# Three float32r passes in the last network's first layer, and sixteen products of zeros in the first step

## The chip, the core and the metric

The kernel runs on one core of a Trainium2 chip. The core has five engines, each with its own instruction queue that it works off in order: TensorE (PE; its weight loads are shown as PEld) multiplies matrices into PSUM; VectorE (DVE) and ScalarE (ACT) work element by element and can read and write PSUM and SBUF; GpSimd (POOL) works in SBUF only; SyncE (SP) only starts transfers. Transfers are started from SP's, ACT's and POOL's queues. Engines wait for each other with semaphores.

The metric is the device time of one execution in microseconds (us), as the median of several runs. The profile comes from one profiled execution.

## The reference

A gated linear attention (a matrix state per head that decays by a gate and takes in one outer product for each token) is followed by a two-layer network with a parametric ReLU. Batch 4, 8 heads, 768 tokens, head size 48; model size 384, inner size 2048; everything in float32.

```python
f = 1.0 / (1.0 + np.exp(-f_logit))
for t in range(S):
    state = f[:, :, t, :, None] * state + np.einsum('bhd,bhe->bhde', k[:, :, t], v[:, :, t])
    y[:, :, t] = np.einsum('bhd,bhde->bhe', q[:, :, t], state)
x = y.transpose(0, 2, 1, 3).reshape(B * S, H * D)      # 3072 x 384
h = x @ w_in                                           # 3072 x 2048
g = np.maximum(h, 0.0) + alpha * np.minimum(h, 0.0)
return g @ w_out                                       # 3072 x 384
```

## The kernel before

The 3072 tokens are cut into 12 steps: six chunks of 128 tokens, and for each chunk two pairs of batch rows (U = 2). A step is an attention part and a network part on 2 x 128 = 256 token columns.

**Attention of a step.** `loaded` fetches q, k, f and v; `scanned`, `gated`, `keyed` and others prepare decayed queries and keys on DVE and ACT; PE then makes score products (`scored` into `raw`, `scored4` into `qu`), products between half chunks (`across` into `off`), the state's increments (`pd`) and the output (`summed` into `py`). The output is copied to `y` and carried by ten transfers into `xT`, the network's input with the model dimension on the partitions (`by_token`; four of the transfers are started by ACT). In the first step there is no earlier state, and its parts (`opening`) are single letters: `r` raw scores, `o` the off products, `O` their copies to `A` by ACT, `k` the transposes `pk`, `K` their copies, `u` quarter scores `qu`, `U` and `H` their placing into `ad` by DVE and ACT, `t` copies to `A`, `y` the output product, `x` the way to `xT`.

**Network of a step.** `network` yields 13 pieces. Eight make the first layer: for each f two tiles of 128 inner rows, each as three products over the 384 model rows (`NK` = 3) of a 128x128 block of `w_in_sb` with 256 columns of `xT`, added up in one PSUM bank `ph` (L716). ACT makes `neg` = relu(-ph) (L721), DVE makes `gate` from it, `om` = 1 - alpha and ph (L723); after every fourth f DVE makes four sums `S` of halves of the gate (`sums`, L800). The other five pieces make the second layer as a 2x2 block product with seven instead of eight block products (`pa`, `pb`, `pc`, `pd`, `pe`, L755), with sums on DVE and ACT (`plus`, L759; L766, L776) and two stores. The step (0, 0) has a plain network instead (`po`, L736).

**PSUM.** The network's banks come from a pool of four (`psn`) that are used in turn: `ph0` of a network takes the bank that `pb` of the network before it had, `ph1` that of `pc`, and so on.

**Weights.** `w_in` and `w_out` arrive as raw pieces of 768 words a partition (five `raw` buffers), are converted by ACT (`a`, `b`; four `lead` buffers) and joined by DVE (`w`, `v`) in the first steps.

**Order.** PE, DVE and ACT get their instructions in the order of the list ORDER, which `flat` makes out of two strings written by hand: HEAD for the first steps, USUAL for every later one. In USUAL, `S` is a piece of `attend` of step n, `O` its `carry`, `Q` a piece of `prepare` of step n + 1, and `n` a piece of the network of step n - 1, so a network runs one step behind its attention. The last step's network runs alone at the end (USUAL with n = 12, in which only `n` is left). POOL and SP are ordered by a scheduler. Before all of it, 56 small products into the bank `idle` keep PE at work while the first data arrive (L833).

Of the kernel before, what the change touches and what calls it, by code (L numbers as in the profile page):

```python
# [7 lines left out]

F32 = mybir.dt.float32
I16 = mybir.dt.int16  # L10
F16 = mybir.dt.float16
# [3 lines left out]
AF = mybir.ActivationFunctionType  # L15
ALU = mybir.AluOpType

C = 128
DB = 32
MASKED = (1, 0)  # L20

U = 2
CH = 64
NC2 = C // CH
NB = DB // 4
WP = 768
IDLE = 56
RAWS, LEADS = 5, 4
UP = 2.0 ** 16

HEAD = (
# [8 lines left out]
)  # L40
USUAL = "S n2 S n2 O n Q n3 Q S2 n Q S n Q S n Q n Q n"

def flat(head, usual, steps=12):
    out = []
    for word in " ".join(head).split():
        if word in "awbvW":
            out.append((word, None))
        elif word[0] in "01":
            out.append((word[1:], int(word[0])))
        else:  # L50
            out.append((word[0], int(word[1:])))
    for n in range(len(head), steps + 1):
        for key in usual.split():
            for _ in range(int(key[1:] or 1)):
                k = key[0]
                m = n - 1 if k == "n" else n + 1 if k == "Q" else n
                if 0 <= m < steps:
                    out.append(("P" if k == "Q" else k, m))
    return out

ORDER = flat(HEAD, USUAL)


@with_exitstack
def kernel(
# [30 lines left out]
    nc = tc.nc  # L96
    B, NC, _, HP, _ = qT.shape
    DM = v.shape[-1]
    H = 2 * HP
    D = DM // H  # L100
    NF = alpha.shape[1]
    NK = DM // 128
# [18 lines left out]
    const = ctx.enter_context(tc.tile_pool(name="const", bufs=1))  # L121
    work = ctx.enter_context(tc.tile_pool(name="work", bufs=2))
    staging = ExitStack()
    stage = staging.enter_context(tc.tile_pool(name="stage", bufs=1))
    psa = ctx.enter_context(tc.tile_pool(name="psa", bufs=2, space=bass.MemoryType.PSUM))
# [5 lines left out]
    def bank(name):  # L131
        return psn.tile([128, 512], F32, tag="net", name=name)

# [11 lines left out]
    for bp in range(B // U):  # L145
        vs.append(const.tile([128, NC2, U, DM + 16], F32, tag=f"vs{bp}", name=f"vs{bp}"))
        nc.vector.memset(vs[bp], 0.0)

    kr = const.tile([128, W // 4, 4], F32, tag="kr", name="kr")
    nc.gpsimd.memset(kr[:, :, 3:4], 1.0)  # L150
    NS = G * (NB + 1) + 1
    fs = const.tile([128, NS], F32, tag="fs", name="fs")
    nc.gpsimd.memset(fs, 0.0)
    ones = const.tile([128, NS], F32, tag="ones", name="ones")
    nc.gpsimd.memset(ones, 0.0)
    nc.gpsimd.memset(ones[:, 0:NS:NB + 1], 1.0)
    qd = const.tile([128, G, QW], F32, tag="qd", name="qd")


    mraw = const.tile([128, 4, NB, 4], F32, tag="mraw", name="mraw")  # L160
    nc.gpsimd.memset(mraw, 0.0)
    diag = lvl[:, 1].rearrange("p (i r) -> p i r", r=4)
    for d in range(4):
        nc.gpsimd.tensor_copy(mraw[:, d, :, d:4], diag[:, :, 0:4 - d])
    inq = const.tile([128, NB], F32, tag="inq", name="inq")
    nc.vector.tensor_reduce(inq, diag, mybir.AxisListType.X, ALU.add)
    mquad = const.tile([128, UW], F32, tag="mquad", name="mquad")
    nc.gpsimd.memset(mquad, 0.0)
    for m in range(1, NB):
# [3 lines left out]
                              inq[:, 0:n].unsqueeze(2).broadcast_to((128, n, 4)))  # L173
    mhalf = const.tile([128, VW], F32, tag="mhalf", name="mhalf")
    nc.gpsimd.memset(mhalf, 0.0)
    for half in range(2):
        for m in range(1, NQ):
# [3 lines left out]
                                  inq[:, NQ * half:NQ * half + n].unsqueeze(2).broadcast_to((128, n, 4)))  # L181
    ad = const.tile([128, U, 2, HP, DB], F32, tag="ad", name="ad")
    nc.gpsimd.memset(ad, 0.0)


    A = const.tile([128, U, H, C], F32, tag="A", name="A")
    nc.gpsimd.memset(A, 0.0)
    ident = const.tile([128, 128], F32, tag="ident", name="ident")
    make_identity(nc, ident)
# [74 lines left out]
    def loaded(bp, c, x):  # L264

        i = f"{bp}_{c}"
        b0 = U * bp
        loads = nc.gpsimd if bp or c else nc.sync

        def load(name, src):  # L270
            t = work.tile([128, W], F32, tag=name, name=f"{name}_{i}", bufs=1)
            loads.dma_start(out=t.rearrange("p (u x) -> p u x", u=U),
                              in_=src[b0:b0 + U, c].rearrange("u p h t -> p u (h t)"))
            return t

        f = x["f"] = quads(load("f", fT))
        q = load("q", qT)
        x["k"] = load("k", kT)
        for cc in range(NC2):
            t_, _ = halves(cc)  # L280
            loads.dma_start(out=vs[bp][t_, cc, :, 0:DM], in_=v[b0:b0 + U, c, t_].rearrange("u t d -> t u d"))

        nc.scalar.activation(f, f, AF.Sigmoid)
        nc.scalar.copy(kr[:, :, 2:3], f[:, :, 3:4])
        nc.scalar.copy(qd[:, :, 0:DB], q.rearrange("p (g t) -> p g t", t=DB))  # L285
        by32 = "p (g i) r -> p g (i r)"

        def lagged(d):
            nc.vector.tensor_tensor(qdv[d], qdv[d - 1][:, :, :, 1:5 - d],  # L289
                                    f[:, :, 1:5 - d].rearrange("p (g i) r -> p g i r", i=NB), ALU.mult)  # L290

        nc.vector.tensor_tensor(kr[:, :, 1:2], f[:, :, 2:3], f[:, :, 3:4], ALU.mult)
        lagged(1)
        nc.vector.tensor_tensor(kr[:, :, 0:1], f[:, :, 1:2], kr[:, :, 1:2], ALU.mult)
        lagged(2)
        nc.vector.tensor_tensor(fq, f[:, :, 0:1].rearrange(by32, i=NB), kr[:, :, 0:1].rearrange(by32, i=NB), ALU.mult)
        lagged(3)
# [10 lines left out]
    def scanned(bp, c, x):  # L308

        i = f"{bp}_{c}"  # L310
        ps = work.tile([128, NS], F32, tag="ps", name=f"ps_{i}", bufs=1)
        ut = work.tile([128, G * UW], F32, tag="us", name=f"us_{i}", bufs=1)
        if c:
# [14 lines left out]
        nc.vector.tensor_tensor_scan(ps, fs, ones, 0.0, ALU.mult, ALU.add)  # L328
        ss = work.tile([128, NS], F32, tag="ss", name=f"ss_{i}", bufs=1)
        nc.vector.tensor_tensor_scan(ss[:, ::-1], fs[:, ::-1], ones[:, ::-1], 0.0, ALU.mult, ALU.add)  # L330
# [8 lines left out]
    def keyed(bp, c, x):  # L339
        i = f"{bp}_{c}"  # L340
        k4 = x["k4"] = work.tile([128, W], F32, tag="k4", name=f"k4_{i}", bufs=1)
        nc.vector.tensor_tensor(k4, x["k"], kr.rearrange("p n r -> p (n r)"), ALU.mult)
        x["k4v"] = by_four(k4.rearrange("p (g t) -> p g t", g=G))
        x["q3"] = work.tile([128, GC, 3, DB], F32, tag="q3", name=f"q3_{i}", bufs=1)
        x["ks"] = work.tile([128, GC, 2, DB], F32, tag="ks", name=f"ks_{i}", bufs=1)
        x["kh"] = work.tile([128, GC, DB], F32, tag="kh", name=f"kh_{i}", bufs=1)
        x["f32"] = x["pre"][:, :, NB:NB + 1]
        x["some"] = slice(0, GC) if c else slice(1, GC, 2)
# [15 lines left out]
    def begun(bp, c, x):  # L364
# [3 lines left out]
        started(0, x)  # L368
        f64 = x["f64"] = work.tile([128, U, H], F32, tag="f64", name=f"f64_{bp}_{c}")
        by64 = x["pre"].rearrange("p (a c j) i -> p a c j i", c=NC2, j=2)  # L370
# [336 lines left out]
    def network(bp, c, x):  # L707
        i = f"{bp}_{c}"
        xT = x["T"]
        plain = (bp, c) == steps[0]  # L710
        for f in range(NH):
            ph = bank(f"ph{f}_{i}")
# [20 lines left out]
        if plain:  # L733
# [11 lines left out]
            return  # L745

        a11, a12, a22 = (lambda f, j=j, u=u: gate[:, f, j, u * C:(u + 1) * C] for j, u in ((0, 0), (1, 0), (1, 1)))
        s1, s2, s3, s4 = (lambda f, n=n: late["S"][:, n, f] for n in range(4))
# [8 lines left out]

        def plus(to, of, by, scale=UP):
            nc.vector.scalar_tensor_tensor(to, of[:, 0:DH], scale, by, ALU.mult, ALU.add)  # L759
# [5 lines left out]
        product(pb, a22, t4)  # L765
        nc.scalar.activation(kept, pa[:, 0:DH], AF.Copy, scale=UP)  # L766
        yield
# [7 lines left out]
        plus(o0[:, DH:DM], pd, u2)  # L775
        nc.scalar.activation(o0[:, 0:DH], pa[:, 0:DH], AF.Copy, scale=UP)  # L776
        yield
        pe = bank(f"pe_{i}")
        product(pe, s4, b22)
        plus(u3, pc, kept)  # L780
        plus(o1[:, 0:DH], pb, u3, -UP)
        plus(o1[:, DH:DM], pd, u3)
# [5 lines left out]

    late = {}

    def sums(fs_):
# [10 lines left out]
    def halves_of_w_out():  # L802

        staging.close()
        pool = ctx.enter_context(tc.tile_pool(name="late", bufs=1))
        late["kt"] = pool
# [14 lines left out]

    idle = bank("idle")

    steps = [(bp, c) for c in range(NC) for bp in range(B // U)]
# [3 lines left out]

    pieces["W"] = halves_of_w_out()

    with tc.manual_schedule(engines={mybir.EngineType.PE, mybir.EngineType.DVE, mybir.EngineType.Activation}):
# [12 lines left out]
        for key, n in ORDER:  # L844
            part = pieces[key] if n is None else run[key, n]
            part() if callable(part) else next(part)


# [53 lines left out]
```

## Time and profile before

| what | value |
|---|---|
| median of 3 runs | 607.08 us (605.29 to 607.75) |
| span of the profiled execution | 604.5 us |
| 0 to 41 us | PE busy 27.5, DVE 32.2, ACT 31.3 us |
| 41 to 546 us | PE 503.0 of 505 us, DVE 447.2, ACT 211.1 |
| 546 to 562 us (second layer of network 10, last transfers to xT) | PE 16.0, DVE 1.8, ACT 1.6 |
| 562 to 583 us (first layer of the last network) | PE 21.0, DVE 9.0, ACT 4.2 |
| 583 to 604.5 us (second layer of the last network) | PE 18.2, DVE 5.5, ACT 1.3 |

The page lists groups of instructions as "line engine op out<-in xcount | busy us, mean ns of one | idle before, releaser". Records of PE overlap, so the distance from one to the next says more than the length of one. An f32 product shows as two records. A line of a timeline is "start us, length us, engine, line, op, xcount [idle before <-who ended it]"; it runs like instructions together.

### The profile page before, as it was taken

To read this page: it belongs to the slowest core of one execution; us is meant where nothing else is said; L and a number is where in the kernel's file an instruction comes from. 1 tells how busy PE (TensorE), PEld (TensorE's weight loads), DVE (VectorE), ACT (ScalarE), POOL (GpSimd) and SP (SyncE) were. 2 spreads that over 40 slices of the span, in tenths; PEclk is the share of its full clock that TensorE was granted. 3 is DMA by queue.
4 is the path that set the end of the run, shared out by engine and by line. 5 is a ranking of instruction groups with operands and counts; after the bars stand their busy time and mean duration, and the time that the engine had idled before them with its cause. 6 is when DMAs were issued, how large, how long until landed. Compare 5 with 4: busy or idle time off the path is not lost.

```text
span 604.5 us, 18724 instructions
## 1 busy us (share of the span) xinstructions
PE 585.7 (97%) x8040; PEld 526.9 (87%) x8040; DVE 495.7 (82%) x997; ACT 249.5 (41%) x478; POOL 62.8 (10%) x117
## 2 busy tenths in 40 slices
PE   5689999999999999999999999999999999999997
PEld 5678768898898899899899899799899899889997
DVE  7799999998898888889889899798798798761351
ACT  5988943712622442452452361262161363232110
POOL 8210010010010010010020020001001000000000
PEclk9999999999999999999999999999999999999999
DMA  8969132324232242232233223303314401201000
GB/s 284 359 209 381 38 88 50 76 62 104 49 88 31 81 101 38 58 104 46 61 87 63 65 54 94 66 37 97 81 36 89 90 3 30 52 2 28 27 1 27
DMA packets 68115, 50.41 MB, mean 83 GB/s; under 512 B 47168, under 2 KB 60608, under 8 KB 68032
## 3 DMA queue, kind: packets, MB, share of 16 engines
q1 hardware_dynamic: 56656, 25.01, 15.6%
q0 software_dynamic: 6864, 22.35, 13.1%
q10 hardware_dynamic: 4512, 1.85, 1.6%
q8 instruction: 64, 1.05, 0.8%
q14 instruction: 19, 0.16, 0.1%
HBM read 36.21 MB, written 4.72 MB: 68 GB/s over the span
## 4 chain that ended last, share of the span: by engine, by line
PE 90%; DVE 4%; ACT 2%; DMA 2%; SPq 1%; issue 1%; DVEq 0%; ACTq 0%
PE ph L716 40%; PE pc L755 9%; PE pa L755 9%; PE pb L755 5%; PE pe L755 4%; PE pd L755 4%; PE py L521 4%; PE po L736 4%; PE qu L498 3%; PE raw L489 3%; PE pd L436 2%; PE off L463 1%; SPq L422 1%; DMA ksn<-kt 1%; DMA f<-in_fT 1%
## 5 line engine op out<-in xcount | busy, mean ns | idle before, releaser
L716 PE MATMUL ph<-xT,w_in_sb 128*128 128x256 f32 x1152 | 257.6, 382 | 0.9 <-issue 0.9
L716 PEld LDWEIGHTS ph<-xT,w_in_sb 128*128 128x128 f32 x1152 | 216.2, 190 | 33.3 <-issue 3.1
L721 ACT ACTIVATE neg<-ph 128x512 f32<-128x512 f32 x96 | 57.0, 596 | 175.2 <-PE ph L716 136.6
L723 DVE SCALAR_TENSOR_TENSOR gate<-neg,om,ph 128x256 f32<-128x256 f32 x192 | 82.5, 477 | 41.3 <-ACT neg L721 41.1
L755 PE MATMUL pc<-t,S 128*128 128x192 f32 x352 | 61.6, 328 | 0.0
L755 PE MATMUL pa<-w_out_sb,gate 128*128 128x192 f32 x352 | 61.1, 327 | 0.0
L755 PEld LDWEIGHTS pa<-w_out_sb,gate 128*128 128x128 f32 x352 | 57.9, 190 | 0.6
L755 PEld LDWEIGHTS pc<-t,S 128*128 128x128 f32 x352 | 57.4, 190 | 0.5
L553 DVE COPY_PREDICATED ad<-mquad,qu 128x224 f32<-128x224 int32 (+6 forms) x140 | 41.9, 299 | 6.2
L506 DVE COPY_PREDICATED ad<-mraw,raw 128x256 f32<-128x256 int32 (+1 forms) x96 | 42.2, 442 | 3.2 <-PE raw L489 0.5
L380 ACT COPY A<-q 48x512 f32<-48x512 f32 x44 | 27.1, 617 | 35.5 <-DVE q L354 35.1
L513 ACT COPY A<-ad 32x256 f32<-32x256 f32 x96 | 38.8, 404 | 1.5
L776 ACT ACTIVATE o<-pa 128x192 f32<-128x192 f32 x11 | 3.6, 330 | 84.2 <-PE pa L755 77.3
L397 DVE TENSOR_TENSOR us<-us,fs 128x768 f32<-128x768 f32 (+5 forms) x60 | 36.6, 611 | 0.1
L759 DVE SCALAR_TENSOR_TENSOR Csum<-pc,Csum 128x192 f32<-128x192 f32 x22 | 7.9, 357 | 29.7 <-PE pc L755 29.3
L800 DVE TENSOR_TENSOR S<-gate 128x512 f32<-128x512 f32 x44 | 30.3, 688 | 0.8
L755 PE MATMUL pb<-t,gate 128*128 128x192 f32 x176 | 30.4, 326 | 0.0
L755 PE MATMUL pe<-w_out_sb,S 128*128 128x192 f32 x176 | 30.4, 326 | 0.0
L755 PE MATMUL pd<-w_out_sb,S 128*128 128x192 f32 x176 | 30.4, 326 | 0.0
L325 ACT COPY us<-qd 128x256 f32<-128x256 f32 x48 | 27.0, 672 | 7.4 <-DVE qd L289 4.4
L289 DVE TENSOR_TENSOR qd<-qd,f 128x768 f32<-128x768 f32 (+2 forms) x36 | 27.1, 752 | 3.2 <-ACT qd L285 3.2
L498 PE MATMUL qu<-us,k 48*32 48x112 f32 (+1 forms) x1536 | 26.1, 259 | 3.8 <-ACT ad L633 2.2
(114 smaller groups left out, 743.6 us busy)
## 6 DMA issues: line engine op xcount, KB each, us to landing
w_out_raw<-in_w_out SPq DMA_DIRECT2D x8, 767.8 KB, 8.4
w_in_raw<-in_w_in SPq DMA_DIRECT2D x8, 767.2 KB, 13.0
q<-in_qT POOLq DMA_DIRECT2D x11, 512.0 KB, 4.2
f<-in_fT POOLq DMA_DIRECT2D x11, 512.0 KB, 4.3
k<-in_kT POOLq DMA_DIRECT2D x11, 512.0 KB, 4.7
out<-o SPq DMA_DIRECT2D x24, 192.0 KB, 2.3
vs<-in_v POOLq DMA_DIRECT2D x22, 192.0 KB, 4.7
ksn<-kt SPq DMA_DIRECT2D x80, 32.0 KB, 2.0
```

The source lines that it names most:

```text
L289: nc.vector.tensor_tensor(qdv[d], qdv[d - 1][:, :, :, 1:5 - d], f[:, :, 1:5 - d].rearrange("p (g i) r -> p g i r", i=NB), ALU.mult)
L380: nc.scalar.copy(A[halves(cc)[1], :, par * HP:(par + 1) * HP, CH * cc:CH * (cc + 1)], x["q3"][rows(par)].rearrange("p (u h c) s t -> p u h ...
L397: nc.vector.tensor_tensor(by_four(us[:, :, UO[m]:UO[m] + 4 * n]), by_four(us[:, :, skip:skip + 4 * n]), spread(fq[:, :, 1:1 + n], n), ALU. ...
L498: nc.tensor.matmul(qu[DB * j:DB * (j + 1), par, hp * QS + 4:hp * QS + QL], lhsT=x["k4"][r_, g * DB:(g + 1) * DB], rhs=x["us"][r_, g, 4:QL] ...
L506: nc.vector.copy_predicated(adu[:, :, :, d:4], mraw[:, d, :, d:4].bitcast(I32).unsqueeze(1).broadcast_to((128, H, NB, n)), rv[:, :, QO[d]: ...
L513: nc.scalar.copy(A[s_, u, :, s_], ad[s_, u].rearrange("p r h t -> p (r h) t"))
L553: nc.vector.copy_predicated(ad[:, u, :, :, 4 * m:DB], mquad[:, lo:lo + n].bitcast(I32).unsqueeze(1).unsqueeze(1).broadcast_to((128, 2, HP, ...
L716: nc.tensor.matmul(ph[:, j * T:(j + 1) * T], lhsT=w_in_sb[:, kt, m * 128:(m + 1) * 128], rhs=xT[:, kt], start=(kt == 0 and j == 0), stop=( ...
L721: nc.scalar.activation(neg, phv, AF.Relu, scale=-1.0)
L723: nc.vector.scalar_tensor_tensor(gate[:, m % NH, m // NH], neg[:, j], om[:, m:m + 1], phv[:, j], ALU.mult, ALU.add)
L755: nc.tensor.matmul(to[:, 0:DH], lhsT=of(f), rhs=by(f), start=(f == 0 and not more), stop=(f == NH - 1), skip_group_check=True)
L800: nc.vector.tensor_tensor(to, x_, y_, op)
```

## The change

In the last network's first layer, x and w_in are each split into a high part of 12 bits and a rest. With e = 2^-12, `xh` is (1 + 2^-13) x, which the write as float32r cuts to 12 bits, `xl` = x - xh, `xs` = x - (1 - e) xh; `wh` is -e (1 + 2^-13) w cut in the same way, `wl` = w + wh/e, `ws` = w + (1/e - 1) wh. Three products take the place of one: wh xh + wl xl is added up in the bank, ACT multiplies the bank by e - 1 in place, and ws xs is added to it. All operands are float32r. The result is h scaled by e, and the second layer's factor `up` becomes UP / e.

The order of three parts changes: the last two entries of the order are given by END. `Z` is a piece of the splitting of w_in (one of eight, 768 elements a partition: one ACT, two DVE operations), `X` the first piece of the last network (the splitting of x: one ACT, two DVE operations). The tiles of the splits (`split` pool) take the memory of the attention's tiles, which now lie in a pool `attn` of their own that is closed at the first Z; `stage` and `late` are put on the other side of SBUF.

In the first step, right behind the first score products `0r0`, PE multiplies zeros: four products each of 512, 384, 192 and 128 columns, float32r, into `idle`. The zeros are a copy by POOL of 128x512 elements of `A` into `spare`, which takes a `lead` buffer.

```diff
 USUAL = "S n2 S n2 O n Q n3 Q S2 n Q S n Q S n Q n Q n"
+END = ("S n2 S n2 O n n3 S2 n S n S Z n Z2 n Z X n", "Z n Z n Z n Z n10")
...
-        for f in range(NH):
+        if (bp, c) == steps[-1]:
+            yield from three_passes(i, xT)
+        for f in range(NH) if (bp, c) != steps[-1] else ():
...
+    def gated_bank(f, ph, i, up=1.0):
+        neg = work.tile([128, 2, T], F32, tag="neg", name=f"neg{f}_{i}")
+        phv = ph.rearrange("p (j t) -> p j t", j=2)
+        nc.scalar.activation(neg, phv, AF.Relu, scale=-1.0)
+        for j in range(2):
+            m = f + j * NH
+            nc.vector.scalar_tensor_tensor(gate[:, f, j], neg[:, j], om[:, m:m + 1], phv[:, j], ALU.mult, ALU.add)
+        if f % 4 == 3:
+            sums(slice(f - 3, f + 1))
+
+    def three_passes(i, xT):
+        xh, xl, xs = late["x"]
+        nc.scalar.activation(xh, xT, AF.Copy, scale=ROUND)
+        nc.vector.tensor_tensor(xl, xT, xh.bitcast(F32), ALU.subtract)
+        nc.vector.scalar_tensor_tensor(xs, xh.bitcast(F32), EPS - 1.0, xT, ALU.mult, ALU.add)
+        yield
+        banks = {}
+
+        def passes(f, parts, start, stop):
+            n = 0
+            for of, by in parts:
+                for kt in range(NK):
+                    for j in range(2):
+                        n += 1
+                        nc.tensor.matmul(banks[f][:, j * T:(j + 1) * T], lhsT=late[of, f][:, kt, j], rhs=by[:, kt],
+                                         start=start and n == 1, stop=stop and n == len(parts) * NK * 2,
+                                         skip_group_check=True)
+
+        def last(f):
+            passes(f, (("ws", xs),), False, True)
+            gated_bank(f, banks[f], i)
+
+        for f in range(NH):
+            banks[f] = bank(f"ph{f}_{i}")
+            passes(f, (("wh", xh), ("wl", xl)), True, False)
+            nc.scalar.activation(banks[f], banks[f], AF.Copy, scale=EPS - 1.0)
+            if f:
+                last(f - 1)
+                yield
+        last(NH - 1)
+        yield
+
+    def split_of_w_in():
+        attention.close()
+        pool = ctx.enter_context(tc.tile_pool(name="split", bufs=1))
+        late["x"] = [pool.tile([128, NK, T], F32R, tag=n, name=n) for n in ("xh", "xl", "xs")]
+        for f in range(NH):
+            w = w_in_sb.rearrange("p a (j f n) -> p a j f n", j=2, f=NH)[:, :, :, f]
+            wh, wl, ws = (pool.tile([128, NK, 2, 128], F32R, tag=f"{n}{f}", name=f"{n}{f}") for n in ("wh", "wl", "ws"))
+            late["wh", f], late["wl", f], late["ws", f] = wh, wl, ws
+            nc.scalar.activation(wh, w, AF.Copy, scale=-EPS * ROUND)
+            nc.vector.scalar_tensor_tensor(wl, wh.bitcast(F32), 1.0 / EPS, w, ALU.mult, ALU.add)
+            nc.vector.scalar_tensor_tensor(ws, wh.bitcast(F32), 1.0 / EPS - 1.0, w, ALU.mult, ALU.add)
+            yield
...
+    spare = stage.tile([128, 512], F32R, tag="lead", name="spare", bufs=LEADS)
+    nc.gpsimd.tensor_copy(spare, A.rearrange("p u h t -> p (u h t)")[:, 0:512])
...
+            if (key, n) == ("r0", 0):
+                for m in (512, 384, 192, 128):
+                    for _ in range(4):
+                        nc.tensor.matmul(idle[:, 0:m], lhsT=spare[:, 0:128], rhs=spare[:, 0:m], start=True, stop=True)
```

## The prediction

> **What bounds the kernel now.** I read the page first (busy shares, the chain that ended last, the costliest groups), then the chain in order of time for the start, then the timeline of the two stretches that the change touches.
>
> ```profile
> span 604.5 us, 18724 instructions
> PE 585.7 (97%) x8040; PEld 526.9 (87%) x8040; DVE 495.7 (82%) x997; ACT 249.5 (41%) x478; POOL 62.8 (10%) x117
> ...
> PE 90%; DVE 4%; ACT 2%; DMA 2%; SPq 1%; issue 1%; DVEq 0%; ACTq 0%
> ...
> L716 PE MATMUL ph<-xT,w_in_sb 128*128 128x256 f32 x1152 | 257.6, 382 | 0.9 <-issue 0.9
> ```
>
> TensorE sets the end for 90% of the span, and the first layer (L716) is its largest part. The chain in time shows from where:
>
> ```profile
> 20.49 1.05 PE qu L498 x63
> ...
> 24.70 0.25 ACT ad L633
> ...
> 32.16 3.11 PE py L521 x60
> ...
> 41.12 13.15 PE ph L716 x60
> ```
>
> Up to about 41 us DVE, ACT and PE hand the path to each other; from then on it is PE without a gap. So a delay in the first 41 us goes whole into the end, and at the end a microsecond counts only if PE loses it. The stretch that the change rewrites, from the timeline:
>
> ```profile
> 550.20 4.08 ACTq L533 DMA_DIRECT2D xT<-y  x4
> ...
> 557.08 0.33 ACT L776 ACTIVATE o<-pa 128x192 f32<-128x192 f32 x1 [6.91 <-PE pa L755]
> ...
> 562.08 20.88 PE L716 MATMUL ph<-xT,w_in_sb 128*128 128x256 f32 x96
> ...
> 586.52 0.69 DVE L800 TENSOR_TENSOR S<-gate,S 128x512 f32<-128x512 f32 x1
> ...
> 588.00 2.76 PE L755 MATMUL pc<-t,S 128*128 128x192 f32 x16
> ```
>
> The last first layer is 96 records (two to a product) from 562.08 to the first pa record at 582.80: 20.7 us, 215.8 ns each. DVE, nearly idle from 546 to 564, ends its sums S at 587.2, 0.8 us before pc, which needs them.
>
> **The products.** Out go 48 f32 products (96 x 215.8 ns = 20.7 us); in come 144 float32r products of the same 256 columns. No row shows one. Two rows of single operations lie nearest:
>
> ```profile
> L683 PE MATMUL xt<-y,dense x24: 275/275/348, 36.0 to 38.7; 128*128 128x128 f32 x24
> ...
> L658 PE MATMUL pk<-ident,ks x8: 272/272/273, 57.6 to 58.3; 128*128 128x128 f32 x8
> ```
>
> An f32 number has 24 significant bits, two of the 12-bit parts of the change, so an f32 product is four products of parts; it shows as two records, two products of parts in each. By that a sweep of the columns for one pair of parts is half a record: 108 ns for 256 columns (0.42 a column). Lower end: one sweep, 108; as xt records, which load 128x128 weights each, follow one another every (2.92-0.275)/23 = 115 ns (2.92 is their length together in the timeline), I bound the pace of weights by that and take 115. Upper end: pk has one record a transpose, yet it lasts as long as an xt record of the same columns, so a single operation on f32 data can need a whole record's time: 216 ns. I choose the lower end, because each operand here is one part, where pk moves whole numbers. 144 x 115 = 16.6 us, 4.1 less than before, if nothing waits.
>
> **The splits.** Per Z one ACT copy of 768 elements (0.83 us, between 617 ns for 512 and 1046 for 1024) and two DVE operations wl, ws on 768 elements with two SBUF inputs. TENSOR_TENSOR of 768 takes 954 ns; in a row of such, the next starts some 80 ns before the end (S: 0.69 long, 0.61 apart), so 0.87 (0.81 is the elements' part, (954-684)/256 ns each; twice 0.87 if STT on two SBUF inputs were half as fast, rival 2). Eight Z's and the split of x put 17 x 0.87 + 0.87 = 15.7 us on DVE and 7.5 on ACT; the rescaling of eight banks adds 8 x 0.6 to ACT (row neg, 596). The tiles lie where the attention's lay, whose last reader, py, ends at 549.1: no wait.
>
> Walking the queues: ACT issues transfers until 554.28, so wh0 ends at 555.15; wl0, ws0 end 556.9. ACT then has the output copy (waits for pa, 557.08), so wh1 ends 558.24; wl1, ws1, wl2, ws2 follow until 561.76, then three sums of network 10 that used to run at 559.68 (pb's bank, which ph0 takes, is free at 562.4 instead of 560.4), wl3, ws3, and only then xl, 565.36, xs, 566.23. PE, ready at 562.08, does its first six products at 562.6 and stands until xl: 565.5. This stall of 2.6 us, with 0.5 for the bank, is what the cover of DVE's idle time fails to hide. From there 138 x 0.115 = 15.9 us and 0.3 for the last rescaling give 581.7, against 582.80. DVE, after xs: one sum, eight operations wl/ws (7.0), eight pairs of gates (0.87 each, 7.0), eight sums S (0.63, 5.0), and 0.8 of waiting for the first gate: 586.3, gate 7 at 583.8. pa's last product waits 0.3 for gate 7, so pc starts at 586.95 against 588.00: **-1.05 us**. The engines tie: 10 ns more a product costs 1.3, 0.08 us more a DVE operation 1.0. All after pc is as before.
>
> **The zeros.** POOL first copies 128x512 from A. It reaches this at 11.9, where DVE works through instructions with two SBUF inputs, and the two dense copies just after took 1034 and 1222 ns for 48 columns, ending as DVE's operations did. So it gets in at about 12.15, takes some 0.5 (memset of the same size, 518 ns), and may hold DVE for it (0 to 0.5; I take 0.5, hidden below). PE has ended raw0 by 12.0 and starts the zeros at 12.7. PE is slow here: raw records last 337 ns at 11 us, 234 at 39.6, though the granted clock reads 1.00 in both; py changes from 314 to 222 at 34.6. At half speed (as L626, 1.97 us for 16 records against 1.11) 4 x (512+384+192+128) = 4864 columns take 4.05 us (0.83 ns a column, one sweep), 0.2 more for the weights of the narrow ones: 17.0. Behind them are raw1 (1.1, previously in PE's idle time before 15.71), off and pk. off starts at 18.1 instead of 15.71, +2.4; ACT's copies of off go from 16.91 to 19.3, and what is queued behind them on ACT: a w_in piece, the pk copies, a w_out piece, the copies to A, then ad, which is on the chain at 24.70. ACT idled 1.0 before it, so ad starts at about 26.2: **+1.5**, which goes to the end. DVE's 0.5 lies beside it. POOL's queue moves too: the loads for step 1 go out some 0.5 later, and k's waits until raw1 has read the old k (18 instead of 14); they land 4 to 5 us after, f needed at 25.8, k at 38.9: covered. Lower end -0.6 (zeros early, PE fast, py 2.0 instead of 3.1); upper end, four sweeps for the narrow ones, +4.
>
> [...]
>
> **Sum:** 604.5 - 1.05 + 1.5 = 604.95 for the span; the median of the three runs lies 2.6 above this span, so 607.5.
>
> **Rivals.** (1) A float32r product takes two sweeps. For it: pk. Against: the parts. Then 144 x 216 = 31.1 us, PE alone decides, pc starts 12.5 late: 607.1 + 12.5 + 1.5 = 621. It decides against the change from 122 ns a product on (the walk gives 0 at 124). (2) DVE's wl, ws, xs run at half speed: the trace has STT only with one PSUM input (477 ns for 256 columns, against 418 for TENSOR_TENSOR in SBUF), so nothing excludes it; 17 x 0.8 more makes DVE the bound, +12: 620.6. [...] (3) The zeros hold PE longer: four sweeps for the narrow ones, or a copy that gets in only at 13.3. Place: PE's queue before raw1 and off; from an end of the zeros at 19.7 on it costs more than 0.5% in all; with an end at 20.5, +5: 611. For it: slow PE and no cover but 1.7 us of PE's and 1.0 of ACT's idle time. Against: the sweep count. (4) The head gains (PE fast, -0.6 to -1.1) and DVE's operations are 0.80 (tail -1.9): 604.0.
>
> **How the numbers follow.** A measurement here tells about 0.5% (3.0 us) from no change; the three runs spread by 2.5. Forecast, within 3 us: 43%; (1) 15%, (2) 8%, (3) 19%: slower; (4) and the like: 15%. The range takes the forecast with its own bounds (604.1 to 610.1), (3) and most of (4), and leaves (1) and (2), and a rest of (4), outside: 603.3 to 613.
>
> **What would show it.** Right: L832 records 107 to 117 ns apart; a PE gap near 563 ended by xl; the last gates near 584, pc 1 us earlier against the end; the zeros just after raw0, and ad (L643) 1 to 2 us later than 24.70. Wrong: records 216 apart; wl and ws above 1.5 us; PE standing in the middle of the passes for wl or a rescaled bank; ad not later.

## The result and the profile after

| | median | runs | profiled span |
|---|---|---|---|
| kernel before | 605.88 us (605.02 to 608.60) | 11 | 604.5 us |
| changed kernel | 611.52 us (608.58 to 612.24) | 11 | 610.3 us |

The ratio is 1.0069, 95% interval [1.0050, 1.0088]: slower by 4.2 us, more than the 0.5% that a measurement here can tell from no change. The forecast was 607.5 us, 0.45 more than the median of 607.08 that it started from. A few executions, of several kernels, took 757 to 2094 us; the medians, ratios and intervals here and below are without them.

The page of the changed kernel, with the lines that answer to those of before:

```profile
span 610.3 us, 18898 instructions
PE 590.2 (97%) x8104; PEld 533.3 (87%) x8104; DVE 511.4 (84%) x1015; ACT 261.4 (43%) x495; POOL 63.5 (10%) x118
...
PE 76%; DVE 15%; DMA 2%; ACT 2%; issue 2%; SPq 1%; ACTq 0%; DVEq 0%
...
L728 PE MATMUL ph<-xT,w_in_sb 128*128 128x256 f32 x1056 | 236.5, 382 | 0.0
```

PE's busy time grew by 4.5 us although the last first layer has become shorter, and "issue" (time in which the engine waits for nothing that the profile shows) is now 2% of the chain instead of 1%. The chain in order of time says where one such piece lies:

```profile
21.02 2.89 issue
36.34 3.50 PE py L531 x60
40.50 5.27 PE xt L693 x24
47.29 13.15 PE ph L728 x60
```

The long row of ph starts 6.2 us later than before (41.12). Of that, 1.2 us is taken up again, 1.1 of it at one place: the kernel before waits for a transfer inside its pd products at 435.5 us, and the changed kernel doesn't (the row of ph ahead of them starts at 429.85 before and 435.76 after, the one behind them at 437.85 and 442.69). At the product pe of network 10 the changed kernel is 4.94 us late (564.42 against 559.48). The stretch that was rewritten, PE's timeline:

```profile
564.42 2.76 PE L768 MATMUL pe<-w_out_sb,S 128*128 128x192 f32 x16
567.20 0.95 PE L832 MATMUL ph<-xh,wh 128*128 128x256 f32 x6
570.26 1.03 PE L832 MATMUL ph<-xl,wl 128*128 128x256 f32 x6 [2.11 <-DVE xl L821]
571.09 1.48 PE L832 MATMUL ph<-xh,wh 128*128 128x256 f32 x6
572.37 1.48 PE L832 MATMUL ph<-xl,wl 128*128 128x256 f32 x6
573.65 1.24 PE L832 MATMUL ph<-xs,ws 128*128 128x256 f32 x6
574.73 0.88 PE L832 MATMUL ph<-xh,wh 128*128 128x256 f32 x6
575.45 0.88 PE L832 MATMUL ph<-xl,wl 128*128 128x256 f32 x6
...
593.82 2.76 PE L768 MATMUL pc<-t,S 128*128 128x192 f32 x16
```

Here stands the gap that the prediction expected, ended by xl. The products are one record each: from 574.73 to 575.45 six start, 120 ns apart. But right behind the gap six take 1.28 us (571.09 to 572.37), 213 ns apart. The granted clock, in stretches of 1 us (start and end, length, PE busy and records, granted clock, DMA share, GB/s):

```profile
572.00:573.00 1.00, 1.00 (x6) 0.50 0.54 197
573.00:574.00 1.00, 1.00 (x6) 0.50 0.00 0
574.00:575.00 1.00, 1.00 (x9) 0.77 0.00 0
575.00:576.00 1.00, 1.00 (x11) 1.00 0.00 0
```

So in this execution the clock was halved behind the gap, which makes 18 products take 3.64 us instead of 2.16. From pe to pc, both second-layer rows that have the same length in both kernels, PE needs 29.40 us; before it was 28.52, and the forecast was 27.47. The excess over the forecast's span (610.3 against 604.95, 5.35) is thus 1.93 in the tail (29.40 - 27.47) and 3.44 ahead of it (4.94 against 1.5).

The operations of the splits, by group (busy, mean ns of one, idle before):

```profile
L859 DVE SCALAR_TENSOR_TENSOR wl<-wh,w_in_sb 128x768 fp32r<-128x768 f32 x8 | 7.6, 953 | 3.8 <-ACT wh L858 3.8
L858 ACT ACTIVATE wh<-w_in_sb 128x768 fp32r<-128x768 f32 x8 | 6.5, 836 | 3.1 <-DMA xT<-y 3.1
L821 DVE TENSOR_TENSOR xl<-xT,xh 128x768 fp32r<-128x768 f32 x1 | 1.0, 951 | 0.0
```

wl, a SCALAR_TENSOR_TENSOR with two inputs in SBUF, takes 953 ns, and xl, a TENSOR_TENSOR of the same size, 951: the expected cost.

The first step, PE's timeline:

```profile
12.38 4.96 PE L925 MATMUL idle<-spare 128*128 128x512 f32 x16 [0.39 <-POOL spare L896]
...
20.64 0.38 PE L508 MATMUL qu<-us,k 48*32 48x52 f32 x22 [0.56 <-DVE ad L516]
23.91 0.62 PE L508 MATMUL qu<-us,k 48*32 48x52 f32 x42 [2.89 <-issue]
...
29.01 1.05 PE L508 MATMUL qu<-us,k 48*32 48x52 f32 x64 [2.94 <-DVE ad L516]
...
31.52 1.54 PE L636 MATMUL qu<-us 48*128 48x64 f32 x11 [0.64 <-issue]
```

and ACT's:

```profile
19.14 0.36 ACT L480 COPY A<-off_0a 32x256 f32<-32x256 f32 x1 [2.43 <-PE off_0b L473]
...
24.69 1.23 ACT L390 COPY A<-q 48x512 f32<-48x512 f32 x2
27.18 1.06 ACT L643 COPY ad<-qu 16x128 f32<-16x128 f32 x4 [1.26 <-DVE ad L657]
```

The zeros run from 12.38 to 17.3 (forecast 12.7 to 17.0), off starts at 18.22 (forecast 18.1), ACT's copies of off at 19.14 (forecast 19.3), and ACT has done its queue at 25.92. All this is as forecast. Then ACT idles 1.26 more, because the first qu products stopped after their 22nd record for 2.89 us with nothing named as missing. ad starts at 27.18, 2.5 instead of 1.5 us late. The harm grows behind it: the second qu products start at 29.01, 3.2 us late (25.81 before), a second stop of 0.64 us falls into the L636 products behind them, and py starts at 36.34, 4.2 us late (32.16 before).

### The profile page after: what moved, and what is told of

Same layout as the page of the kernel before. It is cut to its first block, busy times and chain, and to the rows that moved or that the text cites. A ratio compares the mean times of both kernels' runs of the same rounds, so it can differ in the third digit from the quotient of the medians.

```text
span 610.3 us, 18898 instructions
## 1 busy us (share of the span) xinstructions
PE 590.2 (97%) x8104; PEld 533.3 (87%) x8104; DVE 511.4 (84%) x1015; ACT 261.4 (43%) x495; POOL 63.5 (10%) x118
## 3 DMA queue, kind: packets, MB, share of 16 engines
q1 hardware_dynamic: 56656, 25.01, 15.7%
q8 instruction: 64, 1.05, 0.7%
## 4 chain that ended last, share of the span: by engine, by line
PE 76%; DVE 15%; DMA 2%; ACT 2%; issue 2%; SPq 1%; ACTq 0%; DVEq 0%
PE ph L728 33%; PE pa L768 8%; PE pc L768 7%; PE pb L768 4%; PE pd L768 4%; PE py L531 4%; PE pe L768 3%; PE ph L832 3%; PE qu L508 3%; PE raw L499 2%; PE pd L446 1%; DVE ad L516 1%; PE off L473 1%; DVE us L407 1%; SPq L432 1%
## 5 line engine op out<-in xcount | busy, mean ns | idle before, releaser
L728 PE MATMUL ph<-xT,w_in_sb 128*128 128x256 f32 x1056 | 236.5, 382 | 0.0
L728 PEld LDWEIGHTS ph<-xT,w_in_sb 128*128 128x128 f32 x1056 | 198.0, 190 | 29.8 <-issue 2.2
L733 ACT ACTIVATE neg<-ph 128x512 f32<-128x512 f32 x88 | 52.3, 597 | 153.7 <-PE ph L728 109.6
L735 DVE SCALAR_TENSOR_TENSOR gate<-neg,om,ph 128x256 f32<-128x256 f32 x176 | 75.6, 477 | 29.0 <-ACT neg L733 28.8
L508 PE MATMUL qu<-us,k 48*32 48x112 f32 (+1 forms) x1536 | 26.2, 256 | 6.5 <-DVE ad L516 3.5
L531 PEld LDWEIGHTS py<-A,vs 128*64 128x64 f32 x768 | 25.0, 145 | 4.6 <-ACT A L523 2.1
L768 PEld LDWEIGHTS pe<-w_out_sb,S 128*128 128x128 f32 x176 | 28.9, 190 | 0.0
```

The lines of the kernel that those rows point to most:

```text
L508: nc.tensor.matmul(qu[DB * j:DB * (j + 1), par, hp * QS + 4:hp * QS + QL], lhsT=x["k4"][r_, g * DB:(g + 1) * DB], rhs=x["us"][r_, g, 4:QL] ...
L531: nc.tensor.matmul(py[64 * par:64 * par + 64, u, o:o + CH], lhsT=vs[bp][:, cc, u, hd * D:hd * D + 64], rhs=A[:, u, par * HP + hp, CH * cc: ...
L728: nc.tensor.matmul(ph[:, j * T:(j + 1) * T], lhsT=w_in_sb[:, kt, m * 128:(m + 1) * 128], rhs=xT[:, kt], start=(kt == 0 and j == 0), stop=( ...
L733: nc.scalar.activation(neg, phv, AF.Relu, scale=-1.0)
L735: nc.vector.scalar_tensor_tensor(gate[:, m % NH, m // NH], neg[:, j], om[:, m:m + 1], phv[:, j], ALU.mult, ALU.add)
L768: nc.tensor.matmul(to[:, 0:DH], lhsT=of(f), rhs=by(f), start=(f == 0 and not more), stop=(f == NH - 1), skip_group_check=True)
```

## The experiments

### The change taken apart

Theory: two separate costs, the zeros with 4 to 5 us and a tail that gains less than forecast because of the gap, the clock and 120 instead of 115 ns a product. Rival: the tail alone, or the new places of the tiles, makes the whole loss.

**e1_no_zeros**, the changed kernel without the zeros and their copy:

```diff
-    spare = stage.tile([128, 512], F32R, tag="lead", name="spare", bufs=LEADS)
-    nc.gpsimd.tensor_copy(spare, A.rearrange("p u h t -> p (u h t)")[:, 0:512])
...
-            if (key, n) == ("r0", 0):
-                for m in (512, 384, 192, 128):
-                    for _ in range(4):
-                        nc.tensor.matmul(idle[:, 0:m], lhsT=spare[:, 0:128], rhs=spare[:, 0:m], start=True, stop=True)
```

> The changed kernel without the zeros and without POOL's copy of them. Theory (the loss is made in the head by the zeros, and the tail with its three passes costs 0.9 us more than before): the first 41 us are as before, the time is 0.9 us above before, about 606.8, ratio 1.0015. Rival (the zeros are hidden, and the head's later start in the profile is one of the spreads that every kernel's runs show): the time stays near 611, ratio 1.007.

606.85 us, ratio to the kernel before 1.0012 [1.0000, 1.0025]. Its qu rows of the first step run through and ad starts at 24.73. In its profile the tail has the same gap, but the clock stays up behind it (1.00 from 564 to 568 us), and pe to pc is 27.91 us:

```profile
564.34 0.98 PE L832 MATMUL ph<-xl,wl 128*128 128x256 f32 x6 [2.11 <-DVE xl L821]
565.16 0.88 PE L832 MATMUL ph<-xh,wh 128*128 128x256 f32 x6
```

**e12_no_zeros_again**, the same kernel:

> The changed kernel without the zeros a second time, for a second look at its tail. What is open: behind the gap of about 2.1 us ahead of the second passes the granted clock fell to 0.50 in the changed kernel's profile and stayed at 1.00 in the first one without zeros. If the fall is a matter of the single execution, it may appear here (pe to pc 29 to 29.5 us instead of 27.9), and the median is that of the kernel before within 0.25%; if it needs the zeros, pe to pc is 27.9 us again.

606.62 us, ratio 1.0010 [0.9993, 1.0027]. This time the clock fell, to 0.50 from 566 to 569 us (PE's timeline):

```profile
565.86 1.56 PE L832 MATMUL ph<-xl,wl 128*128 128x256 f32 x6 [2.10 <-DVE xl L821]
567.22 1.48 PE L832 MATMUL ph<-xh,wh 128*128 128x256 f32 x6
```

pe to pc is 29.40 us, as in the changed kernel. So the fall doesn't need the zeros; one kernel shows it in one execution and not in another. How often it comes is told by the mean granted clock that is on record for every run: the execution with the fall has 0.997, the one without it 1.000, and a clock of 0.50 for 3.6 of 606 us is just this 0.003. Of the 22 runs of e1 and e12, 16 have 0.997. Their times tell little (606.9 us on average against 606.3, in a spread of over 3 us). The tail is worth -0.6 us without the fall and +0.9 us with it; 16 in 22 make that +0.5 us, which fits the two ratios.

**e2_zeros_only**, the kernel before with the zeros and their copy, as the change has them:

> The kernel before with POOL's copy and the sixteen zero products alone. Theory (head): PE stands after 22 of qu0's records as in the changed kernel, the clock falls to 0.50, and the time is 4.9 us above before, about 610.8, ratio 1.008. Rival (the tail costs it): within 1 us of before.

609.50 us, ratio 1.0062 [1.0037, 1.0088]. Nothing is read from its profile; that of **e6_zeros_again**, the same kernel, can be used:

> The kernel before with the zeros where the change has them, a second time, for a profile that can be read. Both theories: first step as in the changed kernel, off near 18.4 us, PE on issue for 2.5 to 3.5 us inside the first qu products, pe of the eleventh network 4 to 6 us later than in the kernel before; time 4 us over (0.7%).

610.82 us, ratio 1.0085 [1.0054, 1.0116]. PE's timeline shows the stop after the same 22 records:

```profile
21.16 0.38 PE L499 MATMUL qu<-us,k 48*32 48x52 f32 x22
25.14 0.66 PE L499 MATMUL qu<-us,k 48*32 48x52 f32 x42 [3.60 <-issue]
```

(POOL's copy ended later here than in the changed kernel, so the zeros start at 13.85 instead of 12.38.) pe of network 10 stands at 564.59, 5.1 us later than before. The zeros make the loss; the rival falls.

### Why the zeros cost more than their delay

PE's record counts suggest what "issue" stands for. Before, PE stops for 0.40 us on issue after 112 idle and 111 raw records, at record 223. In the changed kernel it stops after 112 idle, 16 zeros, 128 raw, 64 off, 8 pk and 22 qu records, at 350, and next near 477. That is a grid of some 127 records. The page has a queue for it (queue, kind: packets, MB, share of the 16 engines):

```profile
q8 instruction: 64, 1.05, 0.7%
```

64 packets of 16.4 KB for 8104 PE records: 127 records a packet, the step of the grid.

The theory: such a packet is a block of PE's instructions, and PE asks for a block when it enters the one before it. Where the zeros delay this, the block comes late. **e9_shift** moves the grid, by 44 records fewer ahead of everything:

```diff
-IDLE = 56
+IDLE = 34
```

> The changed kernel with 34 instead of 56 of the small idle products at its start, 44 records fewer on PE ahead of everything. Instruction theory: PE stands on issue where its record count passes 350, whatever instruction that is; with 44 records fewer that is no longer the 22nd record of the first qu products but the first records of the L636 group behind them, so the qu products of 20.6 us run through (64 records in one row) and a shorter wait on issue, 1 to 2 us, stands ahead of L636; the time falls by 0 to 2 us against the changed kernel. Rival (the wait is one for data of the qu products that the trace does not name): the wait stays after the 22nd qu record, 2 to 3 us long.

PE's timeline:

```profile
20.82 0.81 PE L508 MATMUL qu<-us,k 48*32 48x52 f32 x64 [0.89 <-DVE ad L516]
21.93 0.40 PE L636 MATMUL qu<-us 48*128 48x64 f32 x2 [0.30 <-DVE us L619]
24.38 1.97 PE L636 MATMUL qu<-us 48*128 48x64 f32 x14 [2.05 <-issue]
```

All 64 qu records run through, and the stop comes after two records of the next group, which is record 350 again (68 + 64 + 16 + 64 + 64 + 8 + 64 + 2). So it belongs to the count and not to an operand. The time is 611.96 us, ratio 1.0087 [1.0056, 1.0118], not below the changed kernel: the stop only moved to an instruction that is on the path as well (and a second stop, 1.98 us, lies at record 477, now inside pd).

**e5_zeros_behind** leaves the grid and the work as in e6, and lets PE pass record 223 before the zeros:

```diff
-            if (key, n) == ("r0", 0):
+            if (key, n) == ("r1", 0):
```

> The kernel before with the sixteen zeros, placed behind the second half of the raw products instead of ahead of it: the same work, ending about as late (18.5 to 18.9 us), so off starts at 18.5 to 18.9 as in the changed kernel. Instruction theory: in the changed kernel the 2.89 us that PE stands on issue inside the first qu products come from the zeros delaying the point at which PE crosses instruction record 223, so that the block behind record 350 is asked for too late; here record 223 is crossed near 12.8 us, before the zeros, the block is there in time, qu runs through, and the time is 2 to 3 us over the kernel before (0.4%). Rival, that only the delay of off behind the zeros counts: the stall stays or another wait of that length takes its place, and the time is 4 to 5 us over (0.7%), as with the zeros ahead.

607.03 us, ratio 1.0017 [0.9997, 1.0037], some 4 us better than with the zeros one piece earlier, though off starts at 18.63, as late as in the changed kernel. The qu row runs through, and ad starts at 26.20, ACT's queue being the limit, as the prediction had it:

```profile
21.14 0.81 PE L499 MATMUL qu<-us,k 48*32 48x52 f32 x64 [0.73 <-DVE ad L507]
...
26.20 1.06 ACT L634 COPY ad<-qu 16x128 f32<-16x128 f32 x4
```

The delay of off alone costs less than I expected of it (2 to 3 us): 1.0 us, with the interval from nothing to 2.2. The second qu products start at 26.22 and py at 33.66, 1.5 us late where the changed kernel is 4.2 late; so 2.7 us at py are the stops' doing. The profile is of the slowest of the nine runs (609.0); in it pe of network 10 is 2.8 us late (562.25), as xt too was slow (see below).

The packets themselves can be found in the queue's rows. In the changed kernel the one before the stop is moved from 21.35 us on, in the view of the transfers between 21.3 and 21.4:

```profile
q8 instruction: 1, 0.02, 70.4%
```

| kernel | PE passes record 223 | packet starts | PE goes on at | from packet |
|---|---|---|---|---|
| before | 13.40 | 17.26 | no stop (record 350 at 20.96) | |
| e5_zeros_behind | 13.39 | 16.70 | no stop (record 350 at 21.29) | |
| changed | 17.72 | 21.35 | 23.91 | 2.56 |
| e6_zeros_again | 19.02 | 22.61 | 25.14 | 2.53 |
| e9_shift | 18.23 | 21.84 | 24.38 | 2.54 |
| e7_short_zeros | 16.44 | 20.30 | 22.87 | 2.57 |
| e10_x_early_zeros | 16.69 | 20.35 | 22.90 | 2.55 |

The packet of this block starts 3.3 to 3.9 us after the crossing, and PE goes on 2.5 to 2.6 us behind that: 6.1 to 6.4 us in all, while the DMA engines are full (share 1.03 to 1.05 from 20 to 30 us in the changed kernel, 1.04 from 13 to 20 before). The kernel before needs the block 7.6 us after its crossing. It has about 1 us to spare (20.96 against 17.26 + 2.55), and the zeros take over 4. The short stop of the kernel before at record 223 is of the same kind: its packet starts at 10.95, 2.45 us before PE goes on at 13.40. The way from the crossing to the packet isn't fixed: for the next block, at record 477, it is 5.0 us in the changed kernel (23.91 to 28.94) and 8.2 in e9 (24.38 to 32.57), and PE again goes on 2.6 and 2.5 us behind the packet (31.52, 35.10). Whether the full DMA engines make it long is not shown, as no run here varies the loads.

**e7_short_zeros**, the kernel before with sixteen zeros of 128 columns:

```diff
-                for m in (512, 384, 192, 128):
+                for m in (128, 128, 128, 128):
```

> The kernel before with sixteen zeros of 128 columns each: the same number of instructions, 2.0 us of PE instead of 4.9, so that they and the raw products end by 15.7 us, when off's data is there. Length theory (the harm is that the zeros outlast the time in which PE has nothing to do): off stays at 15.7 to 16.1, the time within 0.2% of the kernel before. Rival, that their presence does it (sixteen more records in the instruction stream, the POOL copy that holds DVE): 0.4% or more over.

609.20 us, ratio 1.0040 [1.0015, 1.0065]. The premise failed: they take 3.67 us (229 ns each instead of the 125 that I had worked out from the column pace), so off starts at 17.06, not by 15.7, and PE stops 1.66 us on issue. It is half the dose with about half the harm, and doesn't tell length from presence; e5, with the same instructions, does: presence alone costs little.

A last part of the loss is PE's clock in the first step. Behind the zeros PE was fast (four pk_0a records in 0.66 us at 18.98, before 1.09), and then granted only 0.50:

```profile
36.00:40.00 4.00, 3.47 (x60) 0.50 0.30 119
40.00:44.00 4.00, 3.50 (x16) 0.50 0.36 100
```

xt took 5.27 us instead of 2.92. In e6 and e5 the clock was low there too (xt 5.19 and 5.05), in e7, e9 and e10 not (2.94, 2.95, 2.94), and e12 and e4, without zeros, had 4.87 and 4.64 at a clock that reads 1.00. So up to 2.3 us of it goes with the execution.

The mean granted clock of each run carries this to the runs without a profile. Of the changed kernel's 11 runs, seven have 0.980 and took 610.8 to 612.2 us, and four have 0.982 to 0.986 and took 608.6 to 610.4. In e5, five runs at 0.985 and 0.986 took 607.0 to 609.0 us, and four at 0.988 and more took 605.4 to 606.4, no more than the kernel before (606.6 beside them). The kernel before lies between 0.997 and 1.000 in all of the 81 runs taken beside the experiments. So the length of the fall differs by execution, but a fall that can be read comes with the zeros (in e7 in six of ten runs, at 0.980 to 0.988, in the other kernels with zeros in all but one), and a longer one goes with some 2 us. Whether the stop for the block sets it off isn't shown; e5, without the stop, has it as well.

As far as single profiles tell, the 4.94 us at pe of network 10 are 2.2 for the stops (564.42 against 562.25 in e5, both with a slow xt), 2.1 for the slow xt (5.05 in e5 against 2.92), and 0.6 for the delay of off, less what is taken up again at pd.

### The gap in the tail

**e3_fill**, e1 with 17 thrown-away products into the free second bank ahead of the second passes, so that PE doesn't stand:

```diff
...
+            if f == 0:
+                passes(f, (("wh", xh),), True, False)
+                banks[1] = bank(f"ph1_{i}")
+                for _ in range(17):
+                    nc.tensor.matmul(banks[1][:, 0:T], lhsT=late["wh", 0][:, 0, 0], rhs=xh[:, 0], start=True, stop=True,
+                                     skip_group_check=True)
+                passes(f, (("wl", xl),), False, False)
...
```

> e1_no_zeros, and 17 products of the same size (wh0 times xh, thrown away) between the first six products and the six that wait for xl: PE's gap of 2.1 us is filled with work that waits for nothing. Theory (the gap lowers the clock): the granted clock stays 1.00 to the end of the passes, products stay 120 ns apart, and pc starts 1.5 us earlier against the start of the passes than in the changed kernel; about 1.5 below e1_no_zeros. Rival (the slow products at 571 to 574.7 have another cause, such as the banks or the rescaling): the same slow stretch is there, and the time is that of e1_no_zeros.

605.70 us, ratio 0.9997 [0.9980, 1.0013]; 0.15% under e1, with intervals that overlap. No gap, clock at 1.00, pe to pc 27.91 us as in e1's undisturbed execution. The times alone are too close to show the gap's harm, but the clocks do: all 11 runs have 0.999 or 1.000, where 16 of the 22 with the gap have 0.997. In the two kernels below that have no gap and no zeros, e4 and e11, it is 0.999 or 1.000 in all 16 runs. So the gap brings the fall, and not the banks or the rescaling, which e3 has too.

**e4_x_early** takes the wait for xl away: the split of x and of the first two blocks is issued earlier, without the zeros:

```diff
-END = ("S n2 S n2 O n n3 S2 n S n S Z n Z2 n Z X n", "Z n Z n Z n Z n10")
+END = ("S n2 S n2 O n n3 S2 n S n S Z2 n X n Z n", "Z2 n Z n Z n Z n10")
```

> e1_no_zeros with another order at the end: two pieces of w_in's split, then the split of x, then the rest, so that xl is made by about 560 and the three sums of network 10 are no longer behind three pieces. Theory (the stall at xl, with the clock's fall behind it, is what eats the gain): no gap, products 120 ns apart throughout, pc 3 us earlier than before against the start of the passes; 2.9 us below before, about 603.0, ratio 0.995. Rival (DVE's 15.7 us of new work is the bound whatever its order): pc at most 1 us earlier than before, 605 or more.

602.88 us, ratio 0.9950 [0.9931, 0.9969]: faster than both kernels. PE goes from pe into the passes without a gap:

```profile
560.12 2.76 PE L768 MATMUL pe<-w_out_sb,S 128*128 128x192 f32 x16
562.59 1.01 PE L832 MATMUL ph<-xh,wh 128*128 128x256 f32 x6
563.43 0.88 PE L832 MATMUL ph<-xl,wl 128*128 128x256 f32 x6
```

pe to pc is 25.28 us, 3.24 less than before. **e11_x_early_again**, the same kernel:

> The fastest kernel so far (no zeros, x split early) a second time, on the same chip as the next one: 602.9, 0.5% under the kernel before.

604.02 us, ratio 0.9960 [0.9940, 0.9980], pe to pc again 25.28 us. The two agree in their intervals: 0.2 to 0.7% faster.

**e10_x_early_zeros**, the changed kernel, zeros and all, with the END of e4:

> The changed kernel, zeros and all, with the split of x and the scaled parts of the first two blocks issued before the last networks' other work, as in the experiment without zeros. Theory (two costs that add: the zeros' 4 to 5 us in the first step, and in the tail the late x with the clock that falls behind its gap): the tail as without the zeros, pe to pc 25.3 us instead of 29.4, no gap ahead of the second passes and the granted clock at 1.00 there; the first step as in the changed kernel; median 4 us under the changed kernel's, 607 to 608, that is 0.2% over the kernel before. Rival, that the clock's fall in the tail comes from the first step or from the execution and not from the gap: the clock falls there all the same, and the median stays within 2 us of the changed kernel's.

The median is 604.69 us, below the 607 to 608 that I expected. The ratio 1.0003 [0.9984, 1.0021] is 0.66% below that of the changed kernel, the 4 us expected, and 0.43% above e11's, 2.6 us for the zeros. pe to pc is 25.28 us with the clock at 1.00. The two costs add, within what the intervals allow. Its ten runs are two groups, six at 604.2 to 604.8 us with a mean clock of 0.986 and 0.988 (the profile is one of them) and four at 606.5 to 607.8 with 0.982 and 0.983, so a median falls into the faster one.

**e8_wide_start**, e4 with the last four idle products wide:

```diff
-        for _ in range(IDLE):
+        for _ in range(IDLE - 4):
             nc.tensor.matmul(idle[0:32, 0:8], lhsT=ones[:, 0:32], rhs=ones[:, 0:8], start=True, stop=True)
+        for _ in range(4):
+            nc.tensor.matmul(idle[:, 0:256], lhsT=ones[:, 0:128], rhs=ones[:, 0:256], start=True, stop=True)
```

> The fastest kernel so far with the last four of its 56 idle products at the start made wide (128 weights columns, 256 columns, 8 records), so that PE works from 7.9 us to the end of the raw products instead of standing 2.6 us; the count of records is the same. If a stretch of some 5 us of dense work raises PE's clock, as behind the sixteen zeros of the changed kernel (where four pk records took 0.66 us at 18.98), off, pk and qu of the first step run faster and the time falls by 0.5 to 2 us; if it is other work (the loads, DVE) that sets the first step's end, as the rows between 15 and 35 us of the kernel before suggest, nothing changes, within 0.2%; if the raw products come late behind the wide ones it costs 0.5 to 1 us.

602.80 us, ratio 0.9955 [0.9935, 0.9975], beside e11's 0.9960 on the same chip: nothing. The raw products got faster (128 records in 1.94 instead of 2.84 us), but off waits for DVE's data and starts at 15.60 as in e11 (15.59), and the granted clock is down to 0.50 from 16 us on (mean of this run 0.983, of e11's 0.999). A faster PE there has nothing to do earlier.

## Why the prediction was right or wrong

- **The products.** The choice of one sweep (108 to 115 ns a product) and not two (216) was right; the two-sweep rival (621) falls. The size was 120 ns and not 115, 0.56 of the 215.8 of an f32 record where the forecast had taken half as its lower end, and this over 138 products is 0.7 us. The forecast's tail was 27.47 us, and the runs show 27.91 where the clock stays up.
- **The splits.** The durations and the walk through the queues were right: gap ended by xl (2.1 us against 2.6), wl and ws 0.87 apart. The rival of half-speed wl and ws (620.6) falls with the 953 ns: that half speed was an assumption no run shows, and xl (951 ns) and wl take the same time.
- **The gap.** I took the stall of 2.6 us as its length and no more. Behind it PE's clock was 0.50 for some 3.6 us in two of the four profiles that have it (the changed kernel and e12; e1 and e9 show no fall), and this costs 1.5 us more (29.40 against 27.91). So the fall differs by execution, and a gap of 2.1 us was enough for it. The forecast of -1.05 us for the tail failed here, and the cure was not to fill the gap but to issue the split of x earlier (-3.24).
- **The zeros.** The step "ad starts at about 26.2: +1.5" failed. Its own working, times of the zeros, off and ACT's queue, was right within 0.3 us, and e5, where only that working applies, has ad at 26.20. It left out PE's instruction blocks: the zeros move the request for one behind them, and PE stands 2.89 us inside the first qu products and 0.64 inside the second. At ad that is 1.0 us more than ACT's queue (27.18 against 26.20), at py 2.7 (36.34 against 33.66), and 2.2 are left at pe of network 10. A low clock to 45 us came on top, 2.3 us on xt; the prediction had PE's speed behind the zeros only as a possible gain. PE was indeed fast there, but no longer when py and xt came.
- **The rivals.** The third (611, zeros that hold PE longer) has the size of the result but not its mechanism: the zeros ended at 17.3, not at 19.7 or later. A cause that I had not named, PE waiting for its own instructions, had left a trace before: 0.40 us on issue at 13.40, with the DMA engines full (share 1.05 from 10 to 14 us). That the result lies inside the range given is luck: the cause is not one that the range was built from, and the outcome held most likely, a time within 3 us of no change, did not come.

## What to carry to other kernels

In a start where transfers fill the DMA engines, count PE's instructions: here sixteen products ahead of record 223 made PE stand 2.89 us at record 350. Before putting filler products ahead of work, find "issue" waits, count the records between them, and ask which block the filler delays. A short wait of PE in a dense stretch can cost more than its own length: here 2.1 us, and 1.5 more where the clock behind it was 0.50. Look for the engine whose queue puts the late operand last, and move that operand forward rather than keep PE busy. Three float32r products of parts in place of an f32 product can pay (0.4 to 0.5% here) once their splits are off the path.

## What the runs showed of the hardware

- Where PE stood for a block of its instructions, it went on 2.45 to 2.6 us after the block's packet began to move (eight stops, in the table and the text behind it). The packet began 3.3 to 3.9 us after PE had entered the block before, in two later cases 5.0 and 8.2 us; in the changed kernel the DMA engines had a share of 1.03 to 1.05 from 20 to 30 us.
- A gap of 2.1 us in dense work of PE goes with a granted clock of 0.50 for some 3.6 us behind it in 16 of 22 runs, read from their mean clock; with the gap filled or gone, in none of 27.
- The granted clock reads 1.00 in the first 34 us of the kernel before although records there are slow (raw 337 ns, later 234); in e12 xt takes 4.87 us at a reading of 1.00, in the kernel before 2.92 at the same reading. In the changed kernel's first step the fall came behind fast records (four pk records in 0.66 us at 18.98; the clock is 0.86 from 22 to 26 us and 0.50 from 26 to 44). So a high read is to be checked by a record's length here.
- float32r products of 256 columns follow one another every 120 ns at a clock of 1.00 and every 213 ns at 0.50 (changed kernel, behind the gap); with 128 columns, at the start, every 229 ns (e7, 16 in 3.67 us), so there something other than the columns sets the pace.
